# Order and issuing engine of the first weight loads, and the length of the last warm-up matmul, in a fused attention and gated MLP kernel

## The chip, the cores and the metric

The kernel runs on one core of a Trainium2 chip. The metric is the time of one execution on the device in microseconds (us); lower is better. Before the change three runs gave 261.2, 261.64 and 262.14 us, a median of 261.64 us. One more execution was taken with the hardware profiler; it took 261.51 us, of which the trace covers a span of 260.3 us.

## What is computed

The input `A_x` has 2048 rows of 512 bf16 numbers. Two branches run on the same rows and are mixed by a gate of each row:

```python
g = sigmoid((x * gate_w).sum(-1, keepdims=True))
a = attention_with_memory(x, wq, wk, wv, wo, beta)   # 32 heads of 16, 4 segments of 512 rows
b = (gelu(x @ w_gate) * (x @ w_up)) @ w_down         # 512 -> 1792 -> 512
return g * a + (1 - g) * b
```

In each segment the attention takes q, k and v as `x @ wq`, `x @ wk` and `x @ wv`, runs a causal softmax inside the segment, and adds the read-out of a memory that sums the segments before it. What matters here is the start: before any attention can run, the first 512 rows of x must be in the core and transposed, then k and q of segment 0 must be projected from them, so `wk` is the first weight that is needed, then `wq`, then the first columns of `w_gate` and `wv`.

## The kernel before

The program is written as tasks (`task`, `dma`, `Task` in the source), each with the data it reads and writes. The order of the tasks on each engine is written out by hand in the table `ORDER` (lines 43 to 147): five strings of names for TensorE (`pe`), ScalarE (`act`), VectorE (`dve`), GpSimd (`pool`) and SyncE (`sp`). The planner (`Sched.schedule`, line 272) walks these five queues with estimated durations. It doesn't change the order; from its estimated times it gives each group of matmuls one of four PSUM banks (`W0` to `W3`). For the first loads it takes their landing times from the table `LANDING` (line 39). `Emitter.plan` and `finalize` then turn the data dependences into semaphore waits: an instruction waits for the counter of the engine that wrote what it reads.

Loads are issued from two engines. SyncE and ScalarE have one queue of DMAs each, named q1 and q10 in the profile; what an engine issues is an instruction in its own stream, so on ScalarE a load's issue stands in line with the activations. Transposing loads (`xdma`, line 600) and all other transfers are issued by SyncE.

The start of the program, by names and lines:

- `tload` (line 617) is one small exponential on ScalarE into the tile `stmp`. The function table is loaded in front of it.
- `x0_0` and `x0_1` (lines 624 to 628) are the two halves of the first 512 rows, 256 KB each, loaded by SyncE into `hT[1]` as they stand.
- `wk` is loaded in three parts (line 621): `w_wk0` and `w_wk1` are rows 0 to 127 and 128 to 255, 128 KB each; `w_wk2` is the other half, 256 KB. `wq` and `wv` are loaded in two halves of 256 KB: `w_wq0`, `w_wq1`, `w_wv0`, `w_wv1`. SyncE issues `w_wk2`, `w_wq1` and `w_wv1` behind `x0_1`; ScalarE issues the other four, `w_wk0`, `w_wk1`, `w_wq0` and `w_wv0`, behind `tload` and without a wait (lines 629 to 631).
- `w_wg0`, the first half of `w_gate` (896 KB, line 632), follows on SyncE. Behind it stand the transposing loads `x1_0` to `x1_3` of the next segment, the gate weight `gwb` and `beta`, and `w_wg1`.
- `warm0` to `warm6` (line 640) are seven matmuls of 512 columns on a constant, whose result nobody reads.
- `x0t..` (line 653) are 16 transposes of 128x128 on TensorE, eight for each half of the rows. `x0ev..` (lines 660 and 661) copy them from PSUM to `xT[0]`, by ScalarE or VectorE; `x0ev0c_0`, on ScalarE, is one of the two copies that the first matmul of k waits for.
- `K0_0` to `K0_3` (lines 723 to 740) are four groups of eight matmuls of 256 columns: two halves of the rows times four blocks of `wk`. TensorE's order is: transposes of the first half, the four matmuls of block 0 with the first half (`w_wk0`), transposes of the second half, the four matmuls of block 1 with the first half (`w_wk1`), blocks 0 and 1 with the second half, then blocks 2 and 3 (`w_wk2`). Three matmuls of `K0_3` stand behind the `Q0` groups.
- `Q0_0` to `Q0_3` follow (four matmuls of 512 columns each; `w_wq0` first, `w_wq1` from the seventh matmul), then the last three of `K0_3`, then the first halves of `G0_2` and `G0_3` (two matmuls each, on the first half of `w_gate`), then `qk0_0A0`, the first scores, which the first large exponential `exp0_0A0` (line 942) on ScalarE reads. From there ScalarE's exponentials of 2048 columns and TensorE's score matmuls take turns on the same four PSUM banks (`psXALL`), and TensorE does other matmuls in between.
- `gmul0` (line 815) on VectorE multiplies x by the gate weight; it needs `gwb`.

Of the kernel before, what the change touches and what calls it, by code (L numbers as in the profile page):

```python
# [7 lines left out]
PE, ACT, DVE, POOL, SP = "pe", "act", "dve", "pool", "sp"  # L8
# [28 lines left out]
DMA_SPARE = 1.6  # L37
OVERLAP = {PE: 0.0, ACT: 0.1, DVE: 0.08, POOL: 0.0, SP: 0.0}
LANDING = {
    "x0_0": 3.8, "w_wk0": 4.15, "x0_1": 5.2, "w_wk1": 5.7, "w_wk2": 6.6, "w_wq0": 7.0, "w_wq1": 8.4, "w_wv0": 9.2,  # L40
    "w_wv1": 10.2, "w_wg0": 12.2, "x1_0": 12.9, "w_gwb": 13.2, "x1_1": 13.8, "w_beta": 14.1, "x1_2": 14.4, "x1_3": 14.8,
}
ORDER = {
# [50 lines left out]
    ),  # L94
    "act": (
# [43 lines left out]
    ),  # L139
# [6 lines left out]
    ),  # L146
}
# [297 lines left out]
def mm_t(n):  # L445
    return max(0.026, n / 2363.0)
# [14 lines left out]
def build(nc, A_x, A_wq, A_wk, A_wv, A_wo, A_beta, B_x, B_w_gate, B_w_up, B_w_down, gate_w, out):  # L461
    with ExitStack() as es:
        return _build(es, nc, A_x, A_wq, A_wk, A_wv, A_wo, A_beta, B_w_gate, B_w_up, B_w_down, gate_w, out)


def _build(es, nc, A_x, A_wq, A_wk, A_wv, A_wo, A_beta, B_w_gate, B_w_up, B_w_down, gate_w, out):
    def sb(name, shape, dtype=BF):
        return es.enter_context(nc.sbuf_tensor(name, shape, dtype))
# [35 lines left out]
    stmp = sb("stmp", [P, 16], F32)  # L504
# [8 lines left out]
    wq = sb("wq", [P, 4, 512])  # L513
    wk = sb("wk", [P, 4, 512])
    wv = sb("wv", [P, 4, 512])
# [22 lines left out]
    def task(name, eng, instrs, **kw):  # L538
        return S.add(Task(name, {eng: instrs}, **kw))
# [31 lines left out]
    def dma(name, eng, out_ap, in_ap, reads, writes, nbytes, issue=0.5, transpose=False, bias=0.0, sm=None,  # L571
            nonc=False, after=()):
        sm = sm if sm is not None else sem("d")

        def f(e):
            if transpose:
                return e.dma_start_transpose(out_ap(), in_ap())
            if nonc:
                with nc.allow_non_contiguous_dma(reason="small vector"):
                    return e.dma_start(out_ap(), in_ap())  # L580
            return e.dma_start(out_ap(), in_ap())
        return task(name, eng, [Instr(f, reads, writes, issue, dma_sem=sm)], bias=bias, nbytes=nbytes, after=after)
# [12 lines left out]
    def wdma(key, eng, dst, src, nbytes, nonc=False, issue=0.5, reads=()):  # L595
        rank[0] -= 20000.0 if rank[0] > 1.0e5 else 20.0
        dma("w_" + str(key), eng, lambda: dst, lambda: src, list(reads), [("w", key)], nbytes, bias=rank[0],
            nonc=nonc, issue=issue)
# [12 lines left out]
    ones = nc.const_aps.tensor(1.0, (P, 512), BF)  # L611
# [12 lines left out]
    for u in range(2):  # L624
        rank[0] -= 20000.0
        dma(f"x0_{u}", SP, lambda u=u: xin[:, 2 * u:2 * u + 2, :],
            lambda u=u: A_x[0, u * 256:(u + 1) * 256, :].rearrange("(p a) d -> p a d", p=P), [],
            [("hT", 1, 2 * u + a) for a in range(2)], 250000, bias=rank[0], issue=0.5)
        for wkey, i, dst, src in wloads[u:u + 1] if u == 0 else wloads[1:]:
            wdma((wkey, i), SP if (wkey, i) in (("wk", 2), ("wq", 1), ("wv", 1)) else ACT, dst, src, 250000,  # L630
                 issue=0.5)
    wdma(("wg", 0), SP, wg[:, :, 0:half], wgr[:, :, 0:half], 790000)
    xdma(1, 0, 2)
    wdma("gwb", SP, gwb[:], gate_w.partition_broadcast(P), 115000)
# [4 lines left out]

    for i in range(7):  # L640
        gw = Grp(banks)
        task(f"warm{i}", PE, [Instr(lambda e, gw=gw: e.matmul(
            gw.f32()[:, :], ones[:, 0:128], ones[:, :], start=True, stop=True),
            [], [gw.key], mm_t(512))], grp=gw, bias=5000.0 - i)
    XB = XALL.bitcast(BF)
    for nm, u, k0, nk, c0, aa in (("0a", 0, 0, 1, 0, (0,)), ("0c", 0, 0, 1, 3584, (1,)), ("0b", 0, 1, 1, 1024, (0, 1)),
                                  ("1", 0, 2, 2, 2048, (0, 1)), ("0a", 1, 0, 1, 3072, (0, 1)),
# [2 lines left out]
        src = XB[:, c0:c0 + 128 * na * nk].rearrange("p (k a c) -> p k a c", k=nk, a=na)  # L650
# [6 lines left out]
        dst = xT[0][:, k0:k0 + nk, 256 * u:256 * u + 256].rearrange("p k (c a) -> p k a c", a=2)[:, :, aa[0]:aa[-1] + 1, :]  # L657
# [6 lines left out]
    for g in range(4):  # L664
# [8 lines left out]
         bias=3000.0)  # L673
# [604 lines left out]
```

## Time and profile before

| | |
|---|---|
| median of three runs | 261.64 us |
| the profiled execution | 261.51 us |
| span of its trace | 260.3 us |
| TensorE busy | 252.8 us, 97% |
| ScalarE busy | 211.3 us, 81% |
| VectorE busy | 186.7 us, 72% |
| GpSimd busy | 105.9 us, 41% |
| DMA, read from and written to HBM | 9.84 MB and 2.10 MB |

The profile names the engines PE (TensorE matmul), PEld (TensorE weight load), DVE (VectorE), ACT (ScalarE), POOL (GpSimd) and SP (SyncE). `SPq` and `ACTq` are the instructions by which SyncE and ScalarE issue a DMA. In the timeline a row has the start in us from the start of the span, the time up to the end of the last of its instructions, the engine, the line, the operation, what is written and read, the count, and in square brackets how long the engine was idle before and what released it. Neighbouring instructions of one kind are merged into a row. In the windows view a row has the stretch, its length, the busy time of each engine with a count, the granted TensorE clock, the busy share of the 16 DMA engines and the GB/s that they moved. "DMA to landing" is the time from the issue of a load to the moment when its data may be used.

### The profile page before, as it was taken

To read this page: it belongs to the slowest core of one execution; us is meant where nothing else is said; L and a number is where in the kernel's file an instruction comes from. 1 tells how busy PE (TensorE), PEld (TensorE's weight loads), DVE (VectorE), ACT (ScalarE), POOL (GpSimd) and SP (SyncE) were. 2 spreads that over 40 slices of the span, in tenths; PEclk is the share of its full clock that TensorE was granted. 3 is DMA by queue.
4 is the path that set the end of the run, shared out by engine and by line. 5 is a ranking of instruction groups with operands and counts; after the bars stand their busy time and mean duration, and the time that the engine had idled before them with its cause. 6 is when DMAs were issued, how large, how long until landed. Compare 5 with 4: busy or idle time off the path is not lost.

```text
span 260.3 us, 10390 instructions
## 1 busy us (share of the span) xinstructions
PE 252.8 (97%) x4645; PEld 126.8 (49%) x4670; DVE 186.7 (72%) x346; ACT 211.3 (81%) x192; POOL 105.9 (41%) x260
## 2 busy tenths in 40 slices
PE   7999999999999999999999999999999999999996
PEld 3644445445554664534454563454455445454454
DVE  2398889998998338898987317889898602688574
ACT  4799999999998887979868967889985878777721
POOL 8216767814007264263810251445280044327320
DMA  7962212997013272070004023102001200420002
GB/s 220 309 180 42 59 30 59 252 358 149 3 23 61 44 106 63 12 115 3 3 4 102 4 63 73 33 4 87 0 6 23 81 5 0 108 61 3 3 3 83
DMA packets 33100, 18.43 MB, mean 71 GB/s; under 512 B 21152, under 2 KB 32800, under 8 KB 33056
## 3 DMA queue, kind: packets, MB, share of 16 engines
q1 hardware_dynamic: 32080, 16.96, 27.4%
q10 hardware_dynamic: 976, 0.82, 0.9%
q8 instruction: 36, 0.59, 0.9%
q14 instruction: 8, 0.07, 0.1%
HBM read 9.84 MB, written 2.10 MB: 46 GB/s over the span
## 4 chain that ended last, share of the span: by engine, by line
PE 92%; ACT 3%; DMA 2%; issue 2%; DVE 1%; SPq 0%; ACTq 0%
PE psW L544 33%; PE psW L546 25%; PE psW L1104 14%; PE psXALL L936 9%; PE psW L984 5%; DMA hT<-in_A_x_dram 2%; PE psXALL L546 2%; PE psW L992 1%; ACT ptl L942 1%; PE psXALL L544 1%; ACT pt L942 1%; PE psXALL L855 1%; PE psW L902 1%; DVE hT L1083 0%; PE psXALL L653 0%
## 5 line engine op out<-in xcount | busy, mean ns | idle before, releaser
L942 ACT ACTIVATE pt<-psXALL 128x2048 bf16<-128x2048 f32 x64 | 120.2, 1877 | 24.5 <-PE psXALL L936 23.5
L945 POOL TENSOR_SCALAR_AFFINE_SELECT pt<-pt 128x256 bf16<-128x256 bf16 x128 | 56.1, 448 | 90.1 <-ACT pt L942 85.3
L945 POOL TENSOR_SCALAR_AFFINE_SELECT ptl<-ptl 128x512 bf16<-128x512 bf16 x32 | 23.9, 747 | 48.6 <-ACT ptl L942 47.0
L1083 DVE TENSOR_TENSOR hT<-psW,hT 128x512 bf16<-128x512 f32 x56 | 37.2, 683 | 8.9 <-PE psW L544 6.7
L1104 PE MATMUL psW<-wd,hT 32*128 32x512 bf16 x576 | 35.0, 374 | 0.0
L544 PE MATMUL psW<-xT,wg 128*128 128x512 bf16 x121 | 29.8, 380 | 1.0 <-issue 0.6
L544 PE MATMUL psW<-xT,wu 128*128 128x512 bf16 x118 | 29.4, 380 | 1.3 <-issue 1.3
L998 DVE STREAM_TRANSPOSE tb<-psW 128x512 f32<-128x512 f32 x32 | 22.3, 705 | 8.7 <-PE psW L992 8.5
L936 PE MATMUL psXALL<-qT,kpad 32*128 32x320 bf16 (+3 forms) x512 | 25.6, 272 | 0.4 <-ACT ptl L942 0.2
L546 PE MATMUL psW<-xT,wu 128*32 128x512 bf16 x392 | 24.6, 380 | 0.0
L1133 DVE TENSOR_SCALAR ost<-psW,omgt 128x512 bf16<-128x512 f32 x11 | 8.0, 746 | 23.1 <-PE psW L544 21.9
L1104 PEld LDWEIGHTS psW<-wd,hT 32*128 32x128 bf16 x576 | 18.8, 93 | 10.6
L546 PE MATMUL psW<-xT,wg 128*32 128x512 bf16 x384 | 22.9, 380 | 0.0
L1067 ACT ACTIVATE hT<-psW 128x512 bf16<-128x512 f32 x28 | 15.5, 598 | 7.3 <-PE psW L546 7.1
L936 PEld LDWEIGHTS psXALL<-qT,kpad 32*128 32x128 bf16 x512 | 8.6, 92 | 22.7 <-ACT pt L942 15.9
L984 PE MATMUL psW<-pt,vaug 128*17 128x192 bf16 (+3 forms) x512 | 19.3, 273 | 0.0
L544 PEld LDWEIGHTS psW<-xT,wg 128*128 128x128 bf16 x128 | 11.5, 98 | 14.5 <-issue 1.5
L544 PEld LDWEIGHTS psW<-xT,wu 128*128 128x128 bf16 x126 | 11.2, 98 | 14.3 <-issue 2.1
L984 PEld LDWEIGHTS psW<-pt,vaug 128*17 128x17 bf16 x512 | 12.3, 91 | 10.0 <-issue 0.6
L942 ACT ACTIVATE ptl<-psXALL 128x2048 bf16<-128x2048 f32 x8 | 15.0, 1877 | 1.6 <-PE psXALL L936 1.6
L842 POOL COPY exsT<-exs 32x4 f32<-32x4 f32 x64 | 14.0, 219 | 3.8
L546 PEld LDWEIGHTS psW<-xT,wu 128*32 128x32 bf16 x392 | 10.1, 97 | 9.5 <-issue 0.8
(126 smaller groups left out, 379.8 us busy)
## 6 DMA issues: line engine op xcount, KB each, us to landing
out_dram<-ost SPq DMA_DIRECT2D x15, 128.0 KB, 1.8
wg<-in_B_w_gate_dram SPq DMA_DIRECT2D x2, 896.0 KB, 7.7
wu<-in_B_w_up_dram SPq DMA_DIRECT2D x2, 896.0 KB, 6.7
wd<-in_B_w_down_dram SPq DMA_DIRECT2D x2, 896.0 KB, 7.2
phkt<-in_A_x_dram SPq DMA_DIRECT2D x3, 512.0 KB, 3.9
vlow<-vaug SPq DMA_DIRECT2D x8, 136.0 KB, 2.7
hT<-in_A_x_dram SPq DMA_DIRECT2D x2, 256.0 KB, 3.6
wo<-in_A_wo_dram SPq DMA_DIRECT2D x1, 512.0 KB, 5.6
```

Of the source, the lines that this page charges most:

```text
L544: return e.matmul(view(), lhsT, rhs, start=first, stop=last)
L546: r = e.matmul(view()[c:c + 32, :], lhsT[:, c:c + 32], rhs, start=first, stop=last, tile_position=(0, c))
L842: cross = task(f"exsT{s}", POOL, [Instr(lambda e, g=g, c=c: e.tensor_copy(exsT[sl][32 * g:32 * g + 32, c:16:4], exs[32 * c:32 * c + 32, s4 ...
L936: instrs.append(Instr(lambda e, g=g, lhs=lhs, rhs=rhs, c0=c0, ncol=ncol: e.matmul(X[g][:, c0:c0 + ncol], lhs(32 * g), rhs(32 * g), start=T ...
L942: exp_task(s, f"exp{s}_{t}{name}", [Instr(lambda e: e.activation(dst[:], XALL[:, :].rearrange("p (g c) -> p g c", g=4), ACTF.Exp, scale=AT ...
L945: task(f"msk{s}_{t}{name}", POOL, [Instr(lambda e, view=view, pat=pat, base=base: e.affine_select(out=view, in_=view, compare_op=ALU.is_ge ...
L984: instrs.append(Instr(lambda e, t=t, q=q, kb=kb, slot=slot, c0=c0: e.matmul(gp.f32()[32 * q:32 * q + 17, 128 * kb + 64:512], Vaug[sl][:, k ...
L998: task(f"pvt{s}_{t}_{j}", DVE, [Instr(lambda e: e.transpose(Tb[:, j, :], gp.f32()[:, :]), [gp.key], [("Tb", j)], 0.71)], grp=gp)
L1067: lambda e, g=g, ft=ft, s=s: e.activation(hT[s % 2][:, ft, :], g.f32()[:, :], ACTF.Gelu_apprx_tanh),
L1083: task(f"Um{s}_{ft}", DVE, [Instr(lambda e, g=g, ft=ft: e.tensor_tensor(hT[sl][:, ft, :], g.f32()[:, :], hT[sl][:, ft, :], ALU.mult), [g.k ...
L1104: return Instr(lambda e: e.matmul(gs[tile].f32()[:, :], a[32 * r:32 * r + 32, :], b[32 * r:32 * r + 32, :], start=False, stop=False, tile_ ...
L1133: DVE: [Instr(lambda e: e.tensor_scalar(ost[:], g.f32()[:, :], omgt[:, gt:gt + 1], None, ALU.mult), rd, wr, dve_t(512, ap=True))]}, grp=g))
```

## The change

Three things are edited. `w_wk0` is issued by SyncE, between `x0_0` and `x0_1`; ScalarE issues `w_wk1`, `w_wq0` and `w_wv0` only, and each of these declares that it reads `stmp`, so the first of them waits until the activation of `tload` has ended. The last warm-up matmul has 128 columns instead of 512. The landing times of eight loads in the planner's table are edited to go with it. The order strings of TensorE, VectorE and GpSimd are as before.

```diff
 LANDING = {
-    "x0_0": 3.8, "w_wk0": 4.15, "x0_1": 5.2, "w_wk1": 5.7, "w_wk2": 6.6, "w_wq0": 7.0, "w_wq1": 8.4, "w_wv0": 9.2,
+    "x0_0": 3.5, "w_wk0": 3.85, "x0_1": 4.65, "w_wk1": 4.6, "w_wk2": 5.7, "w_wq0": 6.3, "w_wq1": 7.6, "w_wv0": 8.4,
     "w_wv1": 10.2, "w_wg0": 12.2, "x1_0": 12.9, "w_gwb": 13.2, "x1_1": 13.8, "w_beta": 14.1, "x1_2": 14.4, "x1_3": 14.8,
...
     "act": (
-        "tload w_wk0 w_wk1 w_wq0 w_wv0 x0ev0c_0 x0ev0b_0 x0ev0b_1 x0ev1_1 K0_0even K0_1ev K0_2ev kl0_01 pke0_0 Q0_1ev "
+        "tload w_wk1 w_wq0 w_wv0 x0ev0c_0 x0ev0b_0 x0ev0b_1 x0ev1_1 K0_0even K0_1ev K0_2ev kl0_01 pke0_0 Q0_1ev "
...
     "sp": (
-        "x0_0 x0_1 w_wk2 w_wq1 w_wv1 w_wg0 x1_0 w_gwb x1_1 w_beta x1_2 x1_3 w_wg1 gl00 gl11 Vlo0_1 gl10 gl01 pkT0_1 "
+        "x0_0 w_wk0 x0_1 w_wk2 w_wq1 w_wv1 w_wg0 x1_0 w_gwb x1_1 w_beta x1_2 x1_3 w_wg1 gl00 gl11 Vlo0_1 gl10 gl01 "
...
         for wkey, i, dst, src in wloads[u:u + 1] if u == 0 else wloads[1:]:
-            wdma((wkey, i), SP if (wkey, i) in (("wk", 2), ("wq", 1), ("wv", 1)) else ACT, dst, src, 250000,
-                 issue=0.5)
+            late = (wkey, i) in (("wk", 1), ("wq", 0), ("wv", 0))
+            wdma((wkey, i), ACT if late else SP, dst, src, 250000, issue=0.5, reads=[("stmp",)] if late else ())
...
     for i in range(7):
         gw = Grp(banks)
-        task(f"warm{i}", PE, [Instr(lambda e, gw=gw: e.matmul(
-            gw.f32()[:, :], ones[:, 0:128], ones[:, :], start=True, stop=True),
-            [], [gw.key], mm_t(512))], grp=gw, bias=5000.0 - i)
+        n = 128 if i == 6 else 512
+        task(f"warm{i}", PE, [Instr(lambda e, gw=gw, n=n: e.matmul(
+            gw.f32()[:, 0:n], ones[:, 0:128], ones[:, 0:n], start=True, stop=True),
+            [], [gw.key], mm_t(n))], grp=gw, bias=5000.0 - i)
```

6 rows, old and new, of the table ORDER are left out of this document.

## The prediction

> **What bounds the kernel now.** I read the page first, then the chain of waits over the first 30 us, then the timeline of the first 14 us, and last the times to landing of the first loads and the DMA's share by stretches. The page says that TensorE has almost no idle time over the whole span, so time can be won only where it does wait, and a gain there lasts only as long as no other engine or load takes its place.
>
> ```profile
> PE 252.8 (97%) x4645; PEld 126.8 (49%) x4670; DVE 186.7 (72%) x346; ACT 211.3 (81%) x192; POOL 105.9 (41%) x260
> ```
>
> The chain from the start (start, length, what):
>
> ```profile
> 1.27 4.26 DMA hT<-in_A_x_dram
> ...
> 5.57 0.62 PE psXALL L653 x8
> 6.19 2.73 PE psW L544 x25
> ...
> 8.97 3.40 PE psXALL L544 x15
> 12.38 1.19 PE psW L544 x7
> ```
>
> The chain runs through the second half of x: issued at 1.27, landed at 5.53, transposed from 5.57. From there TensorE runs without a gap (k, q, the first gate columns) to 13.57, where the first scores follow, and ScalarE's first large exponential starts at 13.95. So the head is bound by x's landing, and the rest by TensorE and ScalarE in turns. The rows of the timeline behind it:
>
> ```profile
> 0.81 1.28 ACT L617 ACT_TABLE_LOAD   x1 [0.81 <-PEq L1263]
> 0.81 0.86 SPq L581 DMA_DIRECT2D hT<-in_A_x_dram  x2
> 0.85 3.15 PE L642 MATMUL psW<-const-bfloat16-1.0 128*128 128x512 bf16 x7 [0.85 <-PEq L1263]
> 0.87 0.89 ACTq L581 DMA_DIRECT2D wk<-in_A_wk_dram  x2
> 1.72 0.43 SPq L581 DMA_DIRECT2D wk<-in_A_wk_dram  x1
> 1.79 0.46 ACTq L581 DMA_DIRECT2D wq<-in_A_wq_dram  x1
> 2.10 0.20 ACT L617 ACTIVATE stmp<-const-bfloat16-1.0 128x1 f32<-128x1 bf16 x1
> 2.27 0.49 ACTq L581 DMA_DIRECT2D wv<-in_A_wv_dram  x1
> 3.22 0.49 SPq L581 DMA_DIRECT2D wg<-in_B_w_gate_dram  x1
> 3.37 0.63 PE L642 MATMUL psW<-const-bfloat16-1.0 128*128 128x512 bf16 x1
> 3.83 0.64 PE L653 MATMUL psXALL<-ident,hT 128*128 128x128 bf16 x8
> 4.17 0.63 ACT L660 ACTIVATE xT<-psXALL 128x128 bf16<-128x128 bf16 x2 [1.86 <-PE psXALL L653]
> 4.58 0.60 PE L544 MATMUL psW<-xT,wk 128*128 128x256 bf16 x4
> 5.33 0.57 SPq L581 DMA_DIRECT2D gwb<-in_gate_w_dram  x1
> 5.57 0.62 PE L653 MATMUL psXALL<-ident,hT 128*128 128x128 bf16 x8 [0.40 <-DMA hT<-in_A_x_dram]
> 6.03 2.89 PE L544 MATMUL psW<-xT,wk 128*128 128x256 bf16 x25
> 12.54 1.03 PE L544 MATMUL psW<-xT,wg 128*128 128x512 bf16 x4
> 13.19 1.23 DVE L815 TENSOR_TENSOR hT<-hT,gwb 128x2048 bf16<-128x2048 bf16 x1
> 13.95 1.91 ACT L942 ACTIVATE pt<-psXALL 128x2048 bf16<-128x2048 f32 x1
> ```
>
> And the times to landing, in the order of the tiles hT (two halves of x), wk (three parts), wq (two), the first half of wg, gwb, and of a lone 128 KB transfer late in the kernel:
>
> ```profile
> DMA to landing us min/median/max: 3.0/3.6/4.3
> DMA to landing us min/median/max: 3.2/4.5/5.0
> DMA to landing us min/median/max: 5.2/5.9/6.6
> DMA to landing us min/median/max: 9.0/9.0/9.0
> DMA to landing us min/median/max: 7.7/7.7/7.7
> out_dram<-ost SPq DMA_DIRECT2D x15, 128.0 KB, 1.8
> ```
>
> With the issues of the timeline they give: x0_0 0.81 + 3.0 = 3.8; x0_1 1.27 + 4.3 = 5.57; wk0 0.87 + 3.2 = 4.07; wk1 1.33 + 4.5 = 5.83; wk2 1.72 + 5.0 = 6.72; wq0 1.79 + 5.2 = 7.0; wg0 3.22 + 9.0 = 12.2; gwb 5.33 + 7.7 = 13.0. The first half of w_gate, landed at 12.2, is used at 12.54: **only 0.3 us of slack.** That is the number which decides this change.
>
> **The change, part by part.**
>
> *x0_0 and the warm-up.* How fast the queues moved data (stretch, its length, busy time of each engine, clock, DMA share, GB/s; and packets, MB and share of SyncE's queue q1 and ScalarE's q10):
>
> ```profile
> 1.80:2.60 0.80, 0.80 (x4) 0.24 (x3) 0.00 (x0) 0.50 (x2) 0.60 (x5) 1.00 1.07 207
> 3.20:3.40 0.20, 0.20 (x2) 0.00 (x0) 0.00 (x0) 0.00 (x0) 0.20 (x1) 1.00 1.14 410
> 3.82:5.57 1.75, 1.24 (x13) 0.79 (x13) 1.04 (x2) 0.63 (x2) 1.75 (x2) 1.00 1.05 359
> q10 hardware_dynamic: 2, 0.00, 2.8%
> ```
>
> The q10 row is that of 2.6 to 2.8 us, ScalarE's first packets; until then only x0_0 moved: 207 GB/s x 0.8 us = 166 of its 262 kB. The other 96 kB shared the engines with wk0. At 410 GB/s they take 0.24 us alone and about 0.5 in equal shares, so x0_0 can land some 0.25 earlier: 3.55. Bounds: 3.8 (nothing), and about 3.0 (a lone 128 KB at 1.8 us plus 0.32 for as much again, from 0.81). The last warm-up matmul starts at 3.37 and holds TensorE for its pitch of 0.43 (6 pitches from 0.85 to 3.37 are 0.42 each) to 3.80; with 128 columns a quarter of that, to 3.48. So it no longer hides x0_0, and the transposes start at 3.57 instead of 3.83. ScalarE's copy then wants to run at 3.57 + 0.34 = 3.91.
>
> *The wait.* tload ends at 2.10 + 0.20 = 2.30; I take 2.36 for the first issue behind it, as DVE and ACT rows follow their releasers by some hundredths. Three issues of 0.46 to 0.49 end at 3.78. Queued behind them on ScalarE is that copy, due at 3.91: **hidden by 0.13 us**, and it costs up to 0.2 if x0_0 should land by 3.2. SyncE has one issue more (0.43), so x0_1 is issued at 1.67 and all behind it, wk2, wq1, wv1, wg0, the transposing loads and gwb, 0.43 later than now.
>
> The Trainium skill ("ScalarE: Activation LUTs", What ACT_TABLE_LOAD costs) adds about 1.38 us of drain to the 1.28 of a table load. By it the wait would end near 3.7 instead of 2.3, as an estimate, and every load on ScalarE's queue would be 1.4 us later still. The rows speak against it here: the activation starts at 2.10, right at the table load's end.
>
> *x0_1.* Ahead of its last byte stand x0_0, wk0 and itself, 655 kB, on SyncE's queue alone until wk1's data join at 3.4 to 4.2 (2.36 plus the 1.0 that x0_0's first data took after its issue, or the 1.8 of wk0's). 655 - 166 = 489 kB at 359 GB/s are 1.36 us from 2.6: 3.96; up to 0.3 more for wk1's share; plus some 0.6 from the last data to the landing (x0_0: 3.2 to 3.8). That is 4.56 to 4.9; I take 4.75. TensorE itself is ready at 3.57 + 0.75 (transpose to first k matmul, 3.83 to 4.58) + 4 x 0.109 = 4.76. So the second transposes start at 4.78 instead of 5.57: **0.79 earlier.** Bounds: 4.76 below; above 5.57 + 0.43 = 6.0, if its issue alone moved it.
>
> *wk1.* TensorE wants it after those eight transposes, at 5.24 (now 6.03, landed 5.83). Issued at 2.36, its time to landing is bounded by 1.8 (the lone 128 KB) and 4.5 (its own now, as second of its queue): 4.2 to 6.9. The nearest row is wk0 on the same queue, first of it and beside SyncE's loads: 3.2, so 5.56. Then k goes on at 5.58, 0.45 earlier than now, and not 0.79.
>
> *wk2, wq.* wk2 is wanted ten matmuls later, at 6.3 or more; the bytes ahead of it and its own, some 1.05 MB, leave 0.88 after 2.6, at 359 GB/s until 5.1, landed 5.7: no wait. wq0 at 2.82 + 5.2 = 8.0 is wanted at 8.18 at the earliest; wq1 at 2.6 + 6.6 = 9.2 six matmuls (1.3) later. No cost; their cover is these 0.2 to 0.3 us.
>
> *wg0.* By the head alone TensorE would come to the first gate matmul at 12.54 - 0.45 = 12.09, or at 11.75 with all of the 0.79. But wg0 is the last of 3.0 MB on both queues, and those are the same 3.0 MB as before, moved by the same engines, full from 2.8 us on:
>
> ```profile
> 10.60:10.80 0.20, 0.20 (x3) 0.10 (x1) 0.20 (x2) 0.20 (x2) 0.00 (x0) 1.00 1.41 310
> 11.40:11.60 0.20, 0.20 (x3) 0.08 (x2) 0.00 (x0) 0.20 (x1) 0.00 (x0) 1.00 0.32 51
> ```
>
> Its order within the queues changes, not its end. I keep 12.2 (its later issue at 3.65 is hidden by eight microseconds of queue). So its matmuls start at 12.28 instead of 12.54, and **0.26 us is what remains.** Where the stall at x goes, the wait for wg0 is next.
>
> *Onwards.* From 12.54 to the exponential at 13.95 are 1.41 us of TensorE work and hand-over; it starts at 13.69. ScalarE is free earlier and waits. gwb, at 13.0, comes as late as now and its VectorE product (13.19 now) doesn't move, but nothing of it is on the chain. After that every task waits on tasks, so I carry 0.26 to the end.
>
> Sum: 261.51 - 0.26 = 261.25 for the profiled execution, whose span leaves 1.2 us outside; the same from the median of the runs, which is 0.13 above it, is 261.38. I predict **261.3 us**.
>
> **The rivals.**
>
> *All of it arrives (0.36).* For: between 10.6 and 10.8 the engines still moved 310 GB/s, at 11.4 only 51, so wg0's last part is a tail on a few engines. Should the new order even that out, wg0 lands up to 0.6 earlier, near 11.6, in time for 11.75; and wk1, alone at the head of its queue, may be as quick as x0_0 (1.0 to its first data, not 1.8). Then 0.79 goes through: 260.7 to 260.85, and a little less should later tasks fall better. Against: the bytes are the same.
>
> *wk1 comes late (0.11).* That is the end on the other side: the load that waits for tload's activation becomes what k waits for. At 4.5 us to landing it is there at 6.86, k's second block starts 0.85 later than now, TensorE reaches wg0 at 13.39, and the kernel takes 262.4. It decides from a landing of 6.03 on. For it: nothing on the queue was quicker than 3.2. Against: the 4.5 included wk0 ahead of it.
>
> *The clock stays low (0.08).* The seven warm-up matmuls run at a pitch of 0.42 per 512 columns, the k matmuls behind at 0.109 per 256 ((2.89 - 0.27) / 24), twice as fast by column. So the clock rises about 3.8, 2.95 us after TensorE began (the granted clock in the windows reads 1.00 all along and doesn't show it). With 0.32 us of warm-up less it might miss this. If half speed lasts for another such stretch, to 6.75, transposes and k take twice as long and TensorE is some 1.4 us behind its new plan, 0.6 behind the old one at wg0: 262.1 to 262.2. The Trainium skill says as much ("TensorE: Matmul & The Clock Gate", Part 1 and Part 4): the clock follows activity in free-running windows of 3.4 us, and transposes don't count as busy; by that length it would be 0.8, as an estimate. Against: in the trace the clock rose with 2.95 us of work, less than a window, and TensorE has fewer gaps after the change.
>
> *Banks (0.07).* The edited landing times can give later groups other PSUM banks; either sign, a few tenths of a us.
>
> **How the numbers follow.** The forecast has 0.38; wg0 holds it whatever wk1 does up to 5.7. About 0.3% (0.8 us) is what a measurement of this kernel can tell from no change. Faster by more: 0.34 of the first rival, 0.02 of the banks: 0.36. Slower by more: 0.09 of wk1, 0.04 of the clock, 0.03 of the banks: 0.16. Within: 0.48, the forecast and what is left of the others. The range goes from the first rival, less 0.3 for the runs' own spread, 260.4, to wk1's 262.4.
>
> **What would show it.** Right: transposes at 3.6 and 4.8, k's second block between 5.2 and 5.6, the first gate matmul near 12.3 behind a wait for wg, the large exponential near 13.7. Wrong: no wait ahead of the gate matmuls (the first rival), a wait for wk after 5.3 that is longer than 0.7, a pitch above 0.2 for k, or the 0.26 at 13.7 gone or grown by 60 us.

## The result, and the profile after

The changed kernel is **slower** by 0.68%: a median of 263.23 us in 22 runs against 261.64 us in 22 runs of the kernel before, a ratio of 1.0068 (95% interval 1.0054 to 1.0083). The forecast was 261.3 us, a gain smaller than the 0.3% that it took for noise, and its range ended at 262.4. The profiled execution took 262.23 us, near the lower end of its runs (261.84 to 265.12), so the trace shows the mechanism at its small end. Six of the 22 runs lie between 264.67 and 265.12 with a mean granted TensorE clock of 0.994, all others at 1.0; they are told of again under the clock. Two runs of the experiments that lie over 1.5% above the fastest run of their kernel (266.55 us in e1_move, 266.84 us in e11_full_warm) are left out of the ratios.

The chain of waits of the changed kernel, as shown of the kernel before (start, length, what):

```profile
1.73 4.52 DMA hT<-in_A_x_dram
...
6.29 0.62 PE psXALL L654 x8
6.91 2.73 PE psW L544 x25
9.64 3.45 PE psXALL L544 x16
13.09 1.19 PE psW L544 x7
```

It is the same chain, and each of its steps behind x's landing is 0.67 to 0.72 us later. x's second half still carries it, issued at 1.73 instead of 1.27 and landed at 6.25 instead of 5.53. The rows of the timeline behind it:

```profile
0.82 0.38 SPq L581 DMA_DIRECT2D hT<-in_A_x_dram  x1
1.26 0.41 SPq L581 DMA_DIRECT2D wk<-in_A_wk_dram  x1
1.73 0.42 SPq L581 DMA_DIRECT2D hT<-in_A_x_dram  x1
2.10 0.20 ACT L617 ACTIVATE stmp<-const-bfloat16-1.0 128x1 f32<-128x1 bf16 x1
2.34 0.40 ACTq L581 DMA_DIRECT2D wk<-in_A_wk_dram  x1
3.56 0.90 PE L654 MATMUL psXALL<-ident,hT 128*128 128x128 bf16 x8
3.99 0.67 ACT L661 ACTIVATE xT<-psXALL 128x128 bf16<-128x128 bf16 x2 [1.68 <-PE psXALL L654]
4.40 0.60 PE L544 MATMUL psW<-xT,wk 128*128 128x256 bf16 x4
6.29 0.62 PE L654 MATMUL psXALL<-ident,hT 128*128 128x128 bf16 x8 [1.29 <-DMA hT<-in_A_x_dram]
6.75 2.89 PE L544 MATMUL psW<-xT,wk 128*128 128x256 bf16 x25
13.26 1.03 PE L544 MATMUL psW<-xT,wg 128*128 128x512 bf16 x4
14.67 1.90 ACT L943 ACTIVATE pt<-psXALL 128x2048 bf16<-128x2048 f32 x1
```

The first transposes came 0.27 us earlier (3.83 before), as forecast. Then TensorE waited 1.29 us for x's second half where it had waited 0.40. The second block of k starts at 6.75 (before 6.03), the gate matmuls at 13.26 (12.54), the large exponential at 14.67 (13.95): 0.72 us at each, and 0.72 is also the difference of the two profiled times.

That holds in general. In all 16 profiles of this study (before, after and the 14 experiments) the time less the start of that exponential is 247.54 to 247.58 us. **The head alone decides**, and nothing behind it gives anything back.

What the DMA engines did by stretches (columns as in the prediction; the last two are their busy share and the GB/s that they moved). Both count a packet whole in the stretch in which it begins, so a stretch with slow packets can show a share above 1.00, and the next one nearly none although they are still under way. The kernel before:

```profile
0.85:3.82 2.97, 2.97 (x7) 0.85 (x7) 0.00 (x0) 1.45 (x2) 2.42 (x9) 1.00 0.67 190
3.40:4.60 1.20, 1.08 (x11) 0.52 (x10) 0.40 (x2) 0.43 (x2) 1.20 (x2) 1.00 1.06 353
```

The changed kernel:

```profile
0.85:3.82 2.97, 2.97 (x10) 1.11 (x11) 0.00 (x0) 1.45 (x2) 2.42 (x9) 1.00 0.66 146
3.40:4.60 1.20, 1.20 (x12) 0.95 (x11) 0.40 (x2) 0.61 (x2) 1.20 (x2) 1.00 0.93 69
3.82:5.57 1.75, 1.18 (x12) 0.79 (x9) 1.03 (x2) 0.67 (x2) 1.75 (x2) 1.00 0.67 194
4.00:4.20 0.20, 0.20 (x5) 0.20 (x4) 0.18 (x1) 0.20 (x1) 0.20 (x1) 1.00 0.07 10
```

Between 3.4 and 4.6 us, with x's second half, `wk1` and `wk2` on their way, the engines count as 93% busy and move 69 GB/s; before they moved 353. From 3.82 to 5.57 it is 194 against the 359 of the prediction's row. At the worst place, 3.6 to 3.8 us, SyncE's queue (packets, MB, share of 16 engines) in the kernel before:

```profile
q1 hardware_dynamic: 35, 0.07, 103.0%
```

and in the changed kernel:

```profile
q1 hardware_dynamic: 12, 0.02, 278.2%
```

A third of the packets, and each took much longer: the share times 16 engines times 0.2 us, by the packets, is 0.09 us before and 0.74 us now. From 4.0 to 4.2 us hardly a packet began (share 0.07, 10 GB/s), with x's second half, `wk1` and `wk2` issued and not landed. In the packets of the trace 15 were under way at 4.0 us, and twelve of these had begun between 3.55 and 3.74 and took 0.55 to 1.46 us; at 3.4 us only two were under way. So the engines did not lack work: packets were slow, and others began late. From 1.6 to 5.6 us they moved 0.78 MB against 1.21 MB.

### The profile page after: what moved, and what is told of

The parts are those of the page before. It is cut to its first block, busy times and chain, and to the rows that moved or that the text cites. A ratio compares the mean times of both kernels' runs of the same rounds, so it can differ in the third digit from the quotient of the medians.

```text
span 261.0 us, 10415 instructions
## 1 busy us (share of the span) xinstructions
PE 256.5 (98%) x4670; PEld 127.0 (49%) x4670; DVE 186.7 (72%) x346; ACT 211.3 (81%) x192; POOL 105.9 (41%) x260
## 4 chain that ended last, share of the span: by engine, by line
PE 96%; DMA 2%; ACT 1%; SPq 0%; issue 0%; ACTq 0%
PE psW L544 36%; PE psW L546 26%; PE psW L1105 14%; PE psXALL L937 9%; PE psW L985 6%; DMA hT<-in_A_x_dram 2%; PE psXALL L546 2%; PE psW L993 1%; PE psXALL L544 1%; ACT ptl L943 1%; PE psXALL L856 1%; PE psW L903 1%; SPq L581 0%; PE psXALL L654 0%; ACT obf L1168 0%
## 5 line engine op out<-in xcount | busy, mean ns | idle before, releaser
L544 PE MATMUL psW<-xT,wg 128*128 128x512 bf16 x128 | 31.3, 380 | 0.0
L544 PE MATMUL psW<-xT,wu 128*128 128x512 bf16 x126 | 31.2, 380 | 0.0
```

Of the source, the lines that this page charges most:

```text
L544: return e.matmul(view(), lhsT, rhs, start=first, stop=last)
```

## The experiments

The change has three parts: the move of `wk0` between the halves of x, the wait on ScalarE, the shorter warm-up. The theories, by the letters of the texts: **A**, ScalarE's queue starts late, while SyncE's loads are under way, and its start holds the engines up; **B**, x's second half is slow because it stands third on SyncE's queue, behind `wk0`, whatever ScalarE does; **C**, the shorter warm-up leaves the clock low; **D**, the first reads from x's second half are slow wherever they stand; **E**, what counts is the bytes moved early by both queues together; **W**, a load behind the wait comes late simply because it is issued later; **G**, the third load of SyncE's queue gets its first data only after 4 us. All ratios are to the kernel before on the same chip, with their 95% intervals; the last two columns are starts in us in the profiled execution, one of each kernel (before: 6.03 and 13.95).

| run | ratio | interval | k's second block | exponential |
|---|---|---|---|---|
| e1_move | 1.0039 | 1.0023 to 1.0054 | 7.77 | 15.69 |
| e2_wait | 1.013 | 1.0111 to 1.015 | 8.77 | 17.89 |
| e3_warm | 1.0004 | 0.9991 to 1.0018 | 5.69 | 14.04 |
| e4_all_sp | 1.0022 | 1.0011 to 1.0033 | 6.19 | 14.12 |
| e5_beta_first | 1.0146 | 1.0106 to 1.0185 | 7.87 | 16.53 |
| e6_touch_x | 1.0076 | 1.0046 to 1.0105 | 8.13 | 16.06 |
| e7_x_first | 1.0047 | 1.0027 to 1.0068 | 7.87 | 16.71 |
| e8_wk0_early | 1.0058 | 1.0038 to 1.0078 | 8.22 | 16.16 |
| e9_wait_two | 1.0005 | 0.9995 to 1.0015 | 5.97 | 13.97 |
| e10_x_both | 1.002 | 1.001 to 1.0029 | 6.08 | 14.41 |
| e11_full_warm | 1.0057 | 1.0033 to 1.0082 | 7.91 | 15.85 |
| e12_beta_ahead | 1.0098 | 1.0084 to 1.0113 | 7.69 | 17.01 |
| e13_wg_ahead | 0.9996 | 0.9984 to 1.0007 | 5.89 | 14.00 |
| e14_move_wk1_now | 1.0059 | 1.0039 to 1.008 | 6.77 | 15.27 |

### The parts, one at a time

**The move alone**: the changed kernel without the wait and with the full warm-up.

```diff
-            wdma((wkey, i), ACT if late else SP, dst, src, 250000, issue=0.5, reads=[("stmp",)] if late else ())
+            wdma((wkey, i), ACT if late else SP, dst, src, 250000, issue=0.5, reads=())
...
-        n = 128 if i == 6 else 512
+        n = 512
```

> The move alone: wk0 second on SyncE's queue, ScalarE's three loads without a wait, all seven warm-up matmuls at 512 columns. Theory A (the slow start of ScalarE's queue holds both queues up for about 1.5 us; because of the wait it falls at 3.3 to 4.8 us, alone, where it used to overlap SyncE's own slow start before 2.8): no stretch under 150 GB/s after 3 us, x0_1 landed by 5.2, time 0.2 to 0.6 us below before. Theory B (x0_1 is slow because it stands third on SyncE's queue behind wk0, whatever ScalarE does): x0_1 landed near 6.2 as in the changed kernel, k's second block at 6.7, time 0.5 to 0.9 us above before.

Slower by 0.39%. Its second transposes in the timeline:

```profile
7.31 0.62 PE L654 MATMUL psXALL<-ident,hT 128*128 128x128 bf16 x8 [1.67 <-DMA hT<-in_A_x_dram]
```

x's second half landed at 7.26, later than in the changed kernel, though ScalarE's queue began at 0.87 and no stretch of 0.2 us between 3 and 5 us fell under 236 GB/s. `wk1` was there at 3.94, `wk0` at 4.32, and `wq0`, issued at 1.30 by ScalarE, at 5.03, all ahead of x; of the 16 engines that carry x's second half 11 had ended by 5.75, the last two at 7.24 and 7.26. Two of SyncE's 2 KB packets, begun at 4.42, took 1.64 and 1.67 us. So the move costs without the wait, later and dearer than B had said (6.2), and x can be late without a fall of the rate.

**The wait alone**: the kernel before, with all four loads of ScalarE behind `tload`.

```diff
-                 issue=0.5)
+                 issue=0.5, reads=() if (wkey, i) in (("wk", 2), ("wq", 1), ("wv", 1)) else [("stmp",)])
```

> The wait alone: loads on the engines of before, all four of ScalarE's behind tload's activation, full warm-up. Theory A: the DMA engines fall under 150 GB/s between about 3.2 and 4.7 us as in the changed kernel; wk0, first on ScalarE's queue, lands at 6.2 to 6.6 and k's first matmul waits for it; 1 us or more above before. Theory B: no such stretch, x0_1 landed by 5.2, wk0 at 2.36 + 3.2 = 5.6, so 0 to 0.5 us above before.

Slower by 1.3%, the second largest cost here. x's second half came early, at 4.37, and `wk0` came at 6.85:

```profile
6.98 0.60 PE L544 MATMUL psW<-xT,wk 128*128 128x256 bf16 x4 [2.28 <-DMA wk<-in_A_wk_dram]
8.77 4.08 PE L544 MATMUL psW<-xT,wk 128*128 128x256 bf16 x25 [0.67 <-DMA wk<-in_A_wk_dram]
```

The first load of ScalarE's queue took 4.5 us from an issue at 2.34, where it had taken 3.2 from 0.87.

**The warm-up alone**: the kernel before with `n = 128 if i == 6 else 512`.

> The short last warm-up matmul alone, loads as before. Theory A and B: 3.80 becomes 3.48 on TensorE, x0_0 lands at 3.8 as before, nothing moves: within 0.1 us of before, mean granted clock 1.00 in all runs. Theory C (the shorter warm-up is what lets the clock stay or fall low, in some executions): some runs at a mean granted clock of 0.994 and 1.5 us above the others, as 6 of the changed kernel's 22 have.

No difference: 1.0004. In its profile k's second block starts 0.34 us earlier than before, and yet the exponential doesn't:

```profile
5.69 2.94 PE L544 MATMUL psW<-xT,wk 128*128 128x256 bf16 x25
12.63 1.02 PE L544 MATMUL psW<-xT,wg 128*128 128x512 bf16 x4 [0.22 <-DMA wg<-in_B_w_gate_dram]
```

That is the wait for the first half of w_gate which the prediction put next.

### Which load behind the wait costs

**`wk0` at once, the three others behind `tload`**, in the kernel before.

```diff
-                 issue=0.5)
+                 issue=0.5, reads=[("stmp",)] if (wkey, i) in (("wk", 1), ("wq", 0), ("wv", 0)) else ())
```

> The kernel before with a wait for tload on ScalarE's last three loads only: wk0 is issued at 0.87 as before, wk1, wq0 and wv0 behind the activation; full warm-up. Theories A and D: both queues and both tensors have begun by 2 us, so nothing stands still; x0_1 has the engines to itself from 3.4 us and lands by 4.8, wk0 at 4.0, wk1 at 2.35 + 2.6 to 4.1 = 5.0 to 6.4; the time is within 0.4 us of before, because the first half of w_gate lands at 12.2 whatever k does. A third view, that any wait ahead of these loads costs: 0.8 us or more above before.

Slower by 0.58%, with x untouched (its second half landed at 4.82). k waits for `wk1`:

```profile
8.22 2.90 PE L544 MATMUL psW<-xT,wk 128*128 128x256 bf16 x25 [1.82 <-DMA wk<-in_A_wk_dram]
```

In the trace 15 of the 16 engines had finished `wk1` by 6.45; one finished at 8.18, and that one decides.

**Only `wq0` and `wv0` behind `tload`**, `wk1` at once too.

```diff
-                 issue=0.5)
+                 issue=0.5, reads=[("stmp",)] if (wkey, i) in (("wq", 0), ("wv", 0)) else ())
```

> The kernel before with the wait on wq0 and wv0 alone; wk0 and wk1 are issued by ScalarE at once, full warm-up. Theory E (in these first microseconds one queue's loads often stop for 0.5 to 1.5 us at the start of a load; as long as the other queue holds early loads it fills the gap, so the two queues together have moved 0.95 to 1.0 MB by 5.0 us, and 0.5 to 0.8 where ScalarE's queue starts late): 0.9 MB or more by 5.0 us, x0_1 and wk1 landed by 5.8, time between 0.3 us below and 0.2 above before. Theory W (any load behind tload's wait costs, since it is issued 0.5 to 1 us later): wq0 lands at 8 or later, but is wanted near 8.9: no cost either; only a time of 0.6 us or more above before would speak against both.

No difference: 1.0005. The two runs differ in `wk1` alone, so **it is `wk1` behind the wait that costs**; the wait itself, on two loads that nobody needs soon, is free. W and E both allow that, as the text says.

**The move with `wk1` at once**, `wq0` and `wv0` behind the wait, full warm-up.

```diff
-... reads=[("stmp",)] if late else ())
+... reads=[("stmp",)] if late and wkey != "wk" else ())
```

> wk0 second on SyncE's queue; ScalarE issues wk1 at once and wq0 and wv0 behind the wait; full warm-up. If the move costs by the share that ScalarE's early loads take (they stood ahead of x0_1 in the kernel with the move alone): x0_1 lands by 5.3, wk1 at 4.0 to 4.5, time within 0.3 us of before. If it costs by x0_1's place behind wk0: x0_1 lands at 5.6 or later, with packets of 0.7 us and more after 3.3 us, and the time is 0.4 to 1.5 us above before.

Slower by 0.59%. `wk1` was there at 4.02, x's second half at 6.27:

```profile
6.31 0.62 PE L654 MATMUL psXALL<-ident,hT 128*128 128x128 bf16 x8 [1.05 <-DMA hT<-in_A_x_dram]
```

As in the move alone, x's second half behind `wk0` is late, although two of ScalarE's three loads now come after 2.3 us. Besides, k's third block waited 0.15 us for `wk2`, which landed at 8.1 (6.7 before).

### Why are the loads slow?

**A: everything on SyncE** (changed kernel; order `x0_0 w_wk0 x0_1 w_wk1 w_wk2 w_wq0 w_wq1 w_wv0 w_wv1`).

```diff
-            wdma((wkey, i), ACT if late else SP, dst, src, 250000, issue=0.5, reads=[("stmp",)] if late else ())
+            wdma((wkey, i), SP, dst, src, 250000, issue=0.5)
```

> The changed kernel with every first load on SyncE's queue, in the order x0_0, wk0, x0_1, wk1, wk2, wq0, wq1, wv0, wv1, wg0; ScalarE issues none. Theory A: without ScalarE's queue there is no second slow start: above 300 GB/s from 2.5 us on, x0_1 landed at 4.6 to 4.9, k's second block at 5.2 to 5.5, 0.3 to 0.8 us below before. Theory B: x0_1 lands near 6.2 again, 0.5 us or more above before.

x's second half landed at 5.56 (wait 0.50 us), and between 4.0 and 4.6 us the engines still fell to 92 to 184 GB/s, with no other queue there to start. A falls as the whole cause, and x landed between what A (4.6 to 4.9) and B (6.2) had said. The time, +0.22%, is less than that of the changed kernel.

**A again: `beta`, 8 KB, moved from SyncE to the front of ScalarE's queue** in the changed kernel, so that this queue starts at 0.88.

```diff
-        "tload w_wk1 w_wq0 w_wv0 ...
+        "tload w_beta w_wk1 w_wq0 w_wv0 ...
```

> The changed kernel, with the 8 KB load of beta moved from SyncE to the front of ScalarE's queue, ahead of the wait, so that this queue has its first transfer at 0.9 us. Theory A (what holds the loads up after 3.3 us is the start of ScalarE's queue): no stretch under 150 GB/s between 3.2 and 4.8 us, x0_1 landed by 5.0, time at or below before (261.2 to 261.8). Theory D (the first packets of a load that goes to a region of HBM which nothing has read just before take 0.4 to 1.7 us instead of 0.05 to 0.08, and the loads behind stand still; x0_1 suffers it because wk0 stands between it and x0_0): x0_1's packets of 2 KB still take up to 1 us or more after 3.3 us, x0_1 lands at 5.5 to 6.3, time 262.5 to 263.5.

1.46% slower, x's second half at 6.99. An early start of the queue didn't help; A falls a second time.

**D: a 1 KB read of x's second half, early on ScalarE**, into a tile that isn't used yet (changed kernel).

```diff
+    dma("w_touch", ACT, lambda: ott[0:16, 0:32], lambda: A_x[0, 256:512:16, 0:32], [], [("ott",)], 1024, ...
```

> The changed kernel, with a load of 1 KB (32 numbers of every 16th row of x's second half) on ScalarE's queue ahead of the wait, into a tile that nobody needs then. Theory A as for the kernel with beta first: x0_1 landed by 5.0. Theory D: the same, since the rows of x0_1 have been read near 2 us; so x0_1's packets stay under 0.3 us and it lands by 5.0, while the kernel with beta first still shows slow ones. If x0_1 is slow in both, neither holds.

Slower by 0.76%, x's second half at 6.32, with packets of up to 1.1 us. In this form D falls. In this profile k's second block waited longer for `wk1`, which came at 8.08.

**The halves of x first, then `wk0`** (changed kernel; SyncE's order `x0_0 x0_1 w_wk0`).

```diff
-        "x0_0 w_wk0 x0_1 w_wk2 ...
+        "x0_0 x0_1 w_wk0 w_wk2 ...
```

> The changed kernel with x0_0, x0_1, wk0 in this order on SyncE's queue. Theory D: x0_1 right behind x0_0 lands at 4.3 to 4.6 as in the kernel with the wait alone, wk0 behind it near 4.6 to 5.2; k's first matmul at 4.6 to 5.3, k's second block then waits for wk1, which comes at 6 to 6.5 on ScalarE's queue: time 261.9 to 262.8. Theory A: a stretch under 150 GB/s between 3.3 and 4.8 us, so wk0 lands near 5.5 or later and k starts after that: 262.8 to 264.

x's second half landed at 4.21, the earliest of all runs. Now `wk0` is third, and late: 14 engines by 4.58, two at 5.11 and 6.08.

```profile
6.21 1.01 PE L544 MATMUL psW<-xT,wk 128*128 128x256 bf16 x4 [1.63 <-DMA wk<-in_A_wk_dram]
```

The profiled execution, 264.27 us, is the slowest of its twelve; their median is 262.36, ratio 1.0047. The wait isn't all that made it slow: k's second block ran at half pace, which the granted clock of the windows (third value from the end) doesn't show.

```profile
7.87 3.81 PE L544 MATMUL psW<-xT,wk 128*128 128x256 bf16 x25
8.00:10.00 2.00, 2.00 (x13) 1.44 (x12) 0.00 (x0) 0.86 (x2) 0.04 (x1) 1.00 1.06 378
```

The same 25 matmuls took 2.89 us before. They start 0.21 us apart up to 9.4 us and 0.11 us apart from 9.8 us on. In e5_beta_first it is so up to 9.4 us (3.63 us for the 25).

**E: x's second half on ScalarE's queue at once, all of wk on SyncE's**, `wq0` and `wv0` behind the wait, full warm-up.

```diff
-            dma(f"x0_{u}", SP, lambda ...
+            dma(f"x0_{u}", (SP, ACT)[u], lambda ...
```

> x0_0 on SyncE and x0_1 on ScalarE, both issued at once; SyncE goes on with wk0, wk1, wk2, wq1, wv1, wg0; wq0 and wv0 are issued by ScalarE behind the wait; full warm-up. Theory E: x0_1 lands by 4.4; from 3.4 us SyncE's queue is alone, so 0.6 to 0.8 MB by 5.0 us and wk1 (issued at 1.73) at 5 to 6; k's second block between 5.2 and 6.2. As wg0 then comes no earlier than 12.2, time within 0.3 us of before, or up to 0.6 above if wg0 is late as in the changed kernel. If loads simply land in order of their issue, x0_1 by 4.4 and wk1 by 5.2, and the time is 0 to 0.3 below before.

Both halves of x were there by 4.70, and the kernel is still 0.2% slower: the first half came at 4.32 instead of 3.78, and k waited 0.23 us for `wk2`. By 5.0 us the queues had moved 0.87 MB. Counted so over the runs (before 0.98, e8 0.96, e1 0.95, after 0.57), E does not order the times: e1 and e8 moved nearly as much as the kernel before and are 0.4 and 0.6% slower.

**`beta` at the very front of SyncE's queue**, in the kernel before.

```diff
-        "x0_0 x0_1 w_wk2 ...
+        "w_beta x0_0 x0_1 w_wk2 ...
```

> The kernel before with the 8 KB load of beta at the very front of SyncE's queue, so that x0_0 and x0_1 are its second and third load, still one behind the other, and issued 0.46 us later; ScalarE's as before. Theory G (the third load of SyncE's queue gets its first data only after 4 us): x0_1 lands at 5.6 or later and its packets take up to 1 us. Theory D, in what is left of it (x0_1 is slow only where another tensor stands between the halves): x0_1 lands at 4.8 to 5.6 with no slow packets after 3 us. In both, x0_0 lands at 4.2 to 4.4 instead of 3.8 and the time is 0 to 0.7 us above before.

0.98% slower. `beta` landed at 4.0, x's first half at 5.51 (3.78 before), its second at 6.93. As x's first half was late itself, this doesn't tell the theories of that text apart; it shows that 8 KB put ahead of x can cost 1.7 us at x.

### Two checks on the rest of the sum

**The changed kernel with the full warm-up** (`n = 512`), for C.

> The changed kernel with all seven warm-up matmuls at 512 columns. Theory C (the shorter warm-up makes the slowest runs, with the clock low for one more stretch): no run above 264.4 us, median near 263. The other view (the low clock comes from TensorE standing idle for x0_1 and wk1, whatever the warm-up): runs above 264.4 us are about as frequent as in the changed kernel (6 of 22), median 262.9 to 263.6.

1.0057 against 1.0068 for the changed kernel, with overlapping intervals; of its eight runs two are above 264.4 us here too. So C falls as what makes the slowest runs. Its profile, 263.39 us, lies nearer to the changed kernel's median than that kernel's own, and has the same loads:

```profile
5.97 0.79 PE L654 MATMUL psXALL<-ident,hT 128*128 128x128 bf16 x8 [0.26 <-DMA hT<-in_A_x_dram]
7.91 2.90 PE L544 MATMUL psW<-xT,wk 128*128 128x256 bf16 x25 [1.16 <-DMA wk<-in_A_wk_dram]
```

Here x's second half is only 0.4 us later than before, and `wk1`, at 7.87, ends the wait. So either of the two loads can be the late one, from one execution to the next.

**The first half of w_gate ahead of `wv1`** on SyncE, in the kernel before.

> The kernel before with the first half of w_gate ahead of wv's second half on SyncE's queue, nothing else. If wg0 is the next wait behind x0_1 (the prediction's claim): wg0 lands at about 11.5 instead of 12.2, and the runs in which x0_1 lands early keep their gain: median 0.1 to 0.4 us below before, no run slower for it (wv1, then at 12.2, is wanted at 14.5). If wg0 does not matter: within 0.1 us of before.

It landed at 11.3 instead of 12.2 and the time didn't move: 0.9996. In the kernel before w_gate isn't the bound; whether it would be, were the head faster, rests on the one profile of e3_warm. The profile of this run can't say: x's second half came early, at 4.77, but TensorE was at half pace (0.95 us for the first four k matmuls instead of 0.60) and began k's second block only at 5.89. So even with x on time the 0.79 us of the first rival would not have come through here.

No version beat the kernel before.

## Why the prediction was wrong

*x's first half and the copy: right.* x0_0 landed at 3.52 (forecast 3.55), the transposes began at 3.56 (3.57), ScalarE's issues went from 2.34 (2.36) to 3.74, ahead of the copy at 3.99. The wait ended right behind the activation that started at 2.10. The 1.38 us of drain which the Trainium skill ("ScalarE: Activation LUTs", What ACT_TABLE_LOAD costs) adds to a table load isn't there in this trace.

*x0_1: the step that failed.* Forecast 4.75, upper bound 6.0, measured 6.25; this is the landing that k waited for in the profile. The term "489 kB at 359 GB/s are 1.36 us" took the rate of a stretch in which both queues were well under way and gave it to a moment in which the loads were just beginning; the rows say 146 GB/s to 3.82 and 194 to 5.57. A better rate alone would not have mended the term, since in e1_move the rate held and x came at 7.26: the last of the 16 engines counts, and not the bytes. The upper bound had a like fault: it moved the landing by the issue alone (0.43) and held the time to landing at 4.3. It was 4.5 here, 5.5 in e1_move. By neighbour, over all profiles with x's halves on SyncE and nothing ahead of them there (one execution of each kernel):

| x's second half | landed at | after its issue |
|---|---|---|
| directly behind the first (e7, e2, e13, e3, e8, e9, before) | 4.21 to 5.53 | 2.9 to 4.3 us |
| behind `wk0` (e4, e11, after, e14, e6, e5, e1) | 5.56 to 7.26 | 3.8 to 5.5 us |

The two groups do not overlap, if only just, and their medians, 4.79 and 6.27, are 1.5 us apart. That the place costs is shown; why it costs more than the 0.46 us of the later issue isn't.

*wk1: the second.* Forecast 5.56, measured 6.48, just in time behind the late x (k's second block at 6.75), but 7.87 and waited for in e11_full_warm. The nearest row, `wk0`'s 3.2 us to landing, was that of a load issued at 0.87 while the engines were empty. Issued at 2.34 the first load of this queue took 4.1 (after, e7_x_first), 4.5 (e2_wait), 5.5 (e11_full_warm) and 5.8 us (e8_wk0_early). The rival "wk1 comes late" had the mechanism and its deciding point, 6.03, right; its price, 262.4, rested on a bound of 4.5 us to landing, while e8_wk0_early took 5.8 us and, with x on time, has a median of 263.11. Its chance of 0.11 was far too small.

*Their sum.* e8_wk0_early puts `wk1` behind the wait at 0.58%, e1_move and e14_move_wk1_now put the move at 0.39 and 0.59%, and the change with both costs 0.68%. They don't add, since both loads are wanted at one point, k's second block, and the later one alone counts.

*wg0: "its order within the queues changes, not its end".* It landed at 12.96, not 12.2. The bytes are the same, but the engines, full "from 2.8 us on" before, stood at 77 and 61 GB/s in the slices at 3.4 and 3.8 us. Moving at 360 GB/s from 5.57 to 12.0 instead of 308 they made up only a part. It wasn't waited for: the gate matmuls follow k's last without an idle row. So the 0.26 that the forecast kept could not show.

*The clock: the low clock was real, its cause was another.* e3_warm and e11_full_warm speak against the warm-up as the cause of the six slow runs. What a low clock looks like is in the windows of e2_wait, whose profile has the mean of 0.994 that six runs of the changed kernel have (granted clock is the third value from the end):

```profile
6.00:8.00 2.00, 1.02 (x12) 0.85 (x12) 0.27 (x1) 0.16 (x1) 2.00 (x3) 0.95 1.00 334
8.00:10.00 2.00, 1.33 (x7) 0.89 (x7) 0.17 (x1) 0.88 (x2) 0.05 (x1) 0.50 1.00 363
10.00:12.00 2.00, 2.00 (x15) 1.56 (x13) 0.00 (x0) 0.00 (x0) 0.00 (x0) 0.69 1.62 278
```

After a wait of 2.28 us the clock was 0.50 between 8 and 10 us, and the 25 k matmuls took 4.08 us instead of 2.89. From 3.79, where the transposes take over from the warm-up, to 8.77 TensorE had run only four matmuls that aren't transposes. By the Trainium skill ("TensorE: Matmul & The Clock Gate", Part 1 and Part 4) an idle window of about 3.4 us halves the clock, and transposes don't count as busy in the same way; this row agrees. The three rows make 3.4 us at half clock (0.2, 2.0 and 1.2), and half of 3.4 us in 264 is a mean of 0.994. The profile of e12_beta_ahead, with the same mean, has such a stretch too, behind a wait of 1.63 us for x, though as long a wait in e1_move (1.67) and e8_wk0_early (1.82) brought none:

```profile
8.00:10.00 2.00, 2.00 (x11) 1.38 (x10) 0.00 (x0) 0.67 (x1) 0.04 (x1) 0.50 1.10 356
```

That the six runs of the changed kernel lost their time in the same way, after a longer wait for x or wk, is argued from the equal mean and wasn't seen in a profile. Besides, the sign that the prediction named, a pitch above 0.2 for k, did appear in the second block of e5_beta_first and e7_x_first, where the pitch halved only at 9.4 to 9.8 us; the 3.8 us of the prediction were those of one execution. Both have the shorter warm-up, and in both TensorE had waited for loads. No profile with the full warm-up shows the second block so, apart from the two in which the granted clock fell. Whether the warm-up or the waits did it isn't shown.

*Banks.* The planner gives the same PSUM banks to every group in both kernels, so this rival had no ground.

*The chances.* The forecast and the two largest rivals rested on landing times seen in one place and one execution, and carried them to another place. The bounds of 4.2 to 6.9 for `wk1` were wide, and three profiles still lie beyond them (7.87, 8.08 and 8.18); a landing of 6.03 lies two thirds of the way up, and 0.11 for all beyond it didn't follow from them.

## What to carry to other kernels

A rate that the DMA engines reach when many loads are under way must not be used for the first loads of a kernel: take a load's time to landing from the same place in its queue with the same neighbours, or keep the whole spread as the bound. Where a matmul waits for several early loads, the last engine of the last load counts, so a load that is wanted early should be issued early even if it shares the engines; holding `wk1` back to let x pass cost 0.58%. Waits put on loads that nobody needs soon (`wq0`, `wv0`) were free. A granted clock of 1.00 in the windows isn't proof of full pace: look at the pitch of the matmuls too (e7_x_first).

## What the runs showed of the hardware

- Packets at the start of a load took 0.4 to 1.7 us in many places here, where packets of 1 KB take 0.046 and of 2 KB 0.084 us a little later. The engines count as busy meanwhile and move little (69 GB/s from 3.4 to 4.6 us in the changed kernel). Neither the late start of the other queue (A) nor the first touch of x's second half (D, in the form tried) explains it; **the cause stays open**.
- The 16 engines end one load far apart: `wk1` in e8_wk0_early 15 by 6.45 and one at 8.18 us; x's second half in the changed kernel one at 4.42 and 15 from 5.59 to 6.24.
- In e5_beta_first and e7_x_first TensorE ran the k matmuls 0.21 us apart up to 9.4 us, 0.11 us apart later, with a granted clock of 1.00 in the windows throughout.
- 8 KB ahead of x on SyncE delayed x's first half from 3.78 to 5.51 us (e12_beta_ahead).
